# Attention in quarter tiles of the array, one bank for layer 1's first product, and a new order from re-priced rules

## The chip, the core and the metric

The kernel runs on one core of a Trainium2 chip. The metric is the device time of one execution in microseconds; of several executions the median counts.

## What is computed

Three stages follow each other. The first is a linear attention over B=4 sequences of S=768 tokens, H=8 heads of D=48 channels, with a decay per channel; its output, one row of 384 per token (3072 tokens), goes through two feed-forward layers with 2048 hidden units and different gates:

```python
state = np.zeros((B, H, D, D))
for t in range(S):
    cur = np.einsum('bhd,bhe->bhde', u[None] * kt, vt)
    y[:, :, t] = np.einsum('bhd,bhde->bhe', rt, state + cur)
    state = wt[:, :, :, None] * state + np.einsum('bhd,bhe->bhde', kt, vt)
...
h = x @ w_in;  g = np.maximum(h, 0.0) + alpha * np.minimum(h, 0.0);  x = g @ w_out
...
h = x @ w_in2; g = h * np.clip(h + 3.0, 0.0, 6.0) / 6.0;             out = g @ w_out2
```

All inputs are float32 except the weights, which arrive as float64 and are cut to float32 on the chip.

## The kernel before, in words

**The layers.** A *slot* is one block of 512 tokens (there are 6) with one of 16 blocks of 128 hidden units, so each layer has 96 slots. In a slot TensorE makes h (9 products `h<-xt,w` or `h<-x,w`: three blocks of 128 rows, each as three products of high and low parts, lines 765 to 767), ScalarE reads h into q, VectorE makes the gated value pg (line 808 in layer 1 from h and q, line 812 in layer 2), ScalarE rounds it to g's high part (line 818), VectorE or GpSimd makes the low part (line 821), and TensorE multiplies g with the second weight into three banks acc (9 products). The weights of a layer (16 x 2 pieces of 128x384) are loaded as float64 and taken apart by ScalarE (lines 95, 738) and by VectorE in two steps (wb, lines 98 and 103); the low part w (line 742) goes to VectorE or GpSimd. Layer 1's weights are made during its first block of tokens.

**The attention.** A *third* is 256 tokens of a sequence (there are 12; a sequence has three), a *unit* is a third of one pair of heads (48 units). Head 0 of a pair lies on partitions 0 to 47, head 1 on 64 to 111. For a unit SP loads k, r and w (`un`); VectorE scans w from the right to the products T (line 386), takes a floor of their first column (line 394) and its reciprocal (line 399) and scans to G (line 402); kr (line 423, VectorE or GpSimd) is k times T and r times G. A third also needs r*u*k summed over the channels (rk products, line 332, and the sums p, line 339). The unit's 256 tokens are two chunks of C=128. TensorE's work for a unit comes in two *visits* between the layers' products:

- the first visit makes the scores A (line 477, four 48x128x128 products, one for a chunk and head) and the transposes of k (line 484);
- then ScalarE copies the transposes (kT, line 509), makes four 128x128 diagonals X of p (line 458), and VectorE puts the scores of earlier tokens over X through a mask (line 499, line 494 for some early units);
- the second visit makes y from states and r (line 588, a block-diagonal 112x112 state for each chunk, which ScalarE fills with four 48x48 copies, line 538) and from X and v (lines 595 and 599), and then the products of kT and v for the next unit (lines 516 and 520); VectorE updates the running state Y (line 562).

y goes to the first layer's input xt as a high part (ScalarE, line 635) and a low part (VectorE, line 641).

**Banks.** PSUM has eight: three acc, two h, two for A (with kT's and the states' products behind the scores), one for y.

**The order.** Every step is declared to a planner (`class Plan`) with its engines and the cost on each, a due time in slots, the steps it waits for and the buffers it takes. The planner runs a list schedule on these costs: at each moment the engine that can begin first takes its ready step with the earliest due time. What comes out is the fixed order of each engine's queue. Costs have only this effect: the semaphores come from the dependencies. A step marked `pair=True` on VectorE takes turns with any step on GpSimd (`pair`, under LOCK). Units 0 to 7 (AHEAD) come before the first slot and borrow buffers of the layers; unit n is due U1 = 2 slots after unit n-1. Filler products on TensorE (`warm`) stand where it would idle before the first slot.

## Time and profile before

| what | us |
|---|---|
| median of 3 runs (944.52 to 947.65) | 946.64 |
| the profiled execution | 945.74 |
| its span, first to last instruction | 944.0 |
| TensorE busy | 920.3 |
| VectorE busy | 556.3 |
| ScalarE busy | 530.9 |
| GpSimd busy | 132.3 |

The profiled execution is one run with the hardware's instruction trace. Its span and its own time differ by what lies before the first and behind the last instruction. Busy time of an engine is the time in which it had an instruction; VectorE's instructions overlap their neighbours a little, so a step from start to start is shorter than a duration. TensorE's products overlap each other too: what one costs is the step to the next. A float32 product of the attention appears as two records, one of a layer as one.

### The profile page before, as it was taken

To read this page: it belongs to the slowest core of one execution; us is meant where nothing else is said; L and a number is where in the kernel's file an instruction comes from. 1 tells how busy PE (TensorE), PEld (TensorE's weight loads), DVE (VectorE), ACT (ScalarE), POOL (GpSimd) and SP (SyncE) were. 2 spreads that over 40 slices of the span, in tenths; PEclk is the share of its full clock that TensorE was granted. 3 is DMA by queue.
4 is the path that set the end of the run, shared out by engine and by line. 5 is a ranking of instruction groups with operands and counts; after the bars stand their busy time and mean duration, and the time that the engine had idled before them with its cause. 6 is when DMAs were issued, how large, how long until landed. Compare 5 with 4: busy or idle time off the path is not lost.

```text
span 944.0 us, 13745 instructions
## 1 busy us (share of the span) xinstructions
PE 920.3 (97%) x4914; PEld 743.2 (79%) x4914; DVE 556.3 (59%) x1087; ACT 530.9 (56%) x1266; POOL 132.3 (14%) x132
## 2 busy tenths in 40 slices
PE   7899989999999999999999999999999999999996
PEld 5677767878888788878888888888888888888885
DVE  8999997465655645564369886353353443443432
ACT  5998776565656655665378876363353453443331
POOL 4333234021121201100011130000000000000000
PEclk9999999999999999999999999999999999999998
DMA  8888214122312310110056530060140320500001
GB/s 250 256 268 283 81 52 145 55 79 70 107 64 57 109 55 31 58 64 7 9 186 197 175 111 1 1 200 1 54 147 1 123 79 1 172 30 1 34 1 38
DMA packets 36750, 86.20 MB, mean 91 GB/s; under 512 B 5056, under 2 KB 7488, under 8 KB 36672
## 3 DMA queue, kind: packets, MB, share of 16 engines
q1 hardware_dynamic: 36672, 85.22, 28.8%
q8 instruction: 41, 0.67, 0.3%
q14 instruction: 37, 0.30, 0.1%
HBM read 73.41 MB, written 9.44 MB: 88 GB/s over the span
## 4 chain that ended last, share of the span: by engine, by line
PE 82%; DVE 1%; DMA 0%; POOL 0%; issue 0%; POOLq 0%; DVEq 0%
PE acc L765 13%; PE acc L767 13%; PE acc L766 13%; PE h L765 12%; PE h L767 12%; PE h L766 12%; PE A L477 2%; PE y L595 1%; PE y L588 1%; PE A L484 1%; DMA rk<-in_tok 0%; PE y L599 0%; PE A L516 0%; POOL rk L332 0%; PE A L520 0%; DVE rk L332 0%
## 5 line engine op out<-in xcount | busy, mean ns | idle before, releaser
L765 PE MATMUL acc<-g,w 128*128 128x512 f32 x576 | 228.9, 397 | 0.0
L767 PE MATMUL acc<-g,w 128*128 128x512 f32 x576 | 224.6, 390 | 0.0
L766 PE MATMUL acc<-g,w 128*128 128x512 f32 x576 | 224.5, 390 | 0.0
L818 ACT ACTIVATE g<-pg 128x512 fp32r<-128x512 f32 x192 | 120.6, 628 | 137.7 <-PE acc L767 126.8
L821 DVE TENSOR_TENSOR g<-pg,g 128x512 fp32r<-128x512 f32 x176 | 121.7, 691 | 124.8 <-ACT g L818 124.7
L765 PEld LDWEIGHTS acc<-g,w 128*128 128x128 f32 x576 | 108.1, 188 | 23.4 <-issue 0.4
L767 PEld LDWEIGHTS acc<-g,w 128*128 128x128 f32 x576 | 108.1, 188 | 22.8
L766 PEld LDWEIGHTS acc<-g,w 128*128 128x128 f32 x576 | 108.2, 188 | 21.6 <-DVE g L821 0.3
L812 DVE SCALAR_TENSOR_TENSOR pg<-q,h 128x512 f32<-128x512 f32 x96 | 65.9, 686 | 98.6 <-ACT q L803 98.4
L808 DVE SCALAR_TENSOR_TENSOR pg<-h,q 128x512 f32<-128x512 f32 x96 | 66.1, 688 | 96.4 <-ACT q L801 96.3
L803 ACT ACTIVATE q<-h,three 128x512 f32<-128x512 f32 x96 | 65.8, 685 | 100.5 <-PE h L767 100.3
L765 PE MATMUL h<-xt,w 128*128 128x512 f32 x288 | 116.3, 404 | 1.2 <-ACT w L738 1.1
L767 PE MATMUL h<-xt,w 128*128 128x512 f32 x288 | 113.0, 392 | 0.9 <-POOL w L742 0.7
L766 PE MATMUL h<-xt,w 128*128 128x512 f32 x288 | 112.3, 390 | 0.0
L765 PE MATMUL h<-x,w 128*128 128x512 f32 x288 | 112.0, 389 | 0.0
L766 PE MATMUL h<-x,w 128*128 128x512 f32 x288 | 112.0, 389 | 0.0
L767 PE MATMUL h<-x,w 128*128 128x512 f32 x288 | 112.0, 389 | 0.0
L801 ACT ACTIVATE q<-h,nal 128x512 f32<-128x512 f32 x96 | 65.6, 684 | 73.6 <-PE h L767 71.7
L423 POOL TENSOR_TENSOR kr<-un,tg 112x512 f32<-112x512 f32 (+1 forms) x43 | 43.6, 1016 | 225.5 <-PE y L588 207.3
L765 PEld LDWEIGHTS h<-xt,w 128*128 128x128 f32 x288 | 54.9, 191 | 13.3 <-ACT w L738 2.2
L767 PEld LDWEIGHTS h<-xt,w 128*128 128x128 f32 x288 | 54.0, 188 | 14.1 <-DVE w L742 1.4
L766 PEld LDWEIGHTS h<-x,w 128*128 128x128 f32 x288 | 54.1, 188 | 11.3
(93 smaller groups left out, 1262.7 us busy)
## 6 DMA issues: line engine op xcount, KB each, us to landing
wraw<-in_w SPq DMA_DIRECT2D x64, 384.0 KB, 3.7
un<-in_unit SPq DMA_DIRECT2D x48, 337.3 KB, 3.2
raw<-in_w SPq DMA_DIRECT2D x32, 384.0 KB, 3.9
rk<-in_tok SPq DMA_DIRECT2D x24, 384.0 KB, 4.0
v<-in_vch SPq DMA_DIRECT2D x12, 384.0 KB, 3.1
x2d<-st SPq DMA_DIRECT2D x18, 256.0 KB, 2.1
x2r<-x2d SPq DMA_DIRECT2D x18, 256.0 KB, 4.6
out<-st SPq DMA_DIRECT2D x18, 256.0 KB, 3.5
```

What stands on the lines that cost most here:

```text
L423: eng[e].tensor_tensor(out=u["kr"][:, i].rearrange("p a (c s) -> p a c s", c=2), in0=u["in"][:, 0 : 2 * TH].rearrange("p (a c s) -> p a c ...
L477: nc.tensor.matmul(A[h][:, cs], kr[r0 : r0 + D, 0, cs], kr[r0 : r0 + D, 1, cs], start=True, stop=True,)
L484: nc.tensor.transpose(T[:, c, :], kr[:, 0, c * C : (c + 1) * C], ident[0:PR, 0:PR])
L765: nc.tensor.matmul(ps, whi, xhi, start=start, stop=False, skip_group_check=True)
L766: nc.tensor.matmul(ps, whi, xlo, start=False, stop=False, skip_group_check=True)
L767: nc.tensor.matmul(ps, wlo, xhi, start=False, stop=stop, skip_group_check=True)
L801: nc.scalar.activation(q, k["h"], AF.Relu, scale=nal[:, f : f + 1])
L803: nc.scalar.activation(q, k["h"], AF.Relu, bias=three)
L808: nc.vector.scalar_tensor_tensor(out=p, in0=k["h"], scalar=0.0, in1=k["q"], op0=ALU.max, op1=ALU.subtract)
L812: nc.vector.scalar_tensor_tensor(out=p, in0=k["q"], scalar=6.0, in1=k["h"], op0=ALU.min, op1=ALU.mult)
L818: nc.scalar.activation(k["g"][:, 0], k["p"], AF.Copy)
L821: eng[e].tensor_tensor(out=k["g"][:, 1], in0=k["p"], in1=k["g"][:, 0].bitcast(F32), op=ALU.subtract)
```

## The change

- **Chunks of 64.** A unit's two chunks j are each split into two sub-chunks p of Q=64 tokens. All products of the attention have at most 64 rows and 64 columns of weights, so that head h (rows) and sub-chunk p (output partitions) choose one of four quarters of the array. Scores within a sub-chunk are 64x64; what an earlier sub-chunk gives goes through states. A unit has 8 score products (N=64), 8 products with an identity in place of the transposes (N=48), 8 of keys and values (6 in the last third), 8 of values (N=64) and 8 of states (N=64; 6 in the first third).
- **States.** A half state U (line 621) and the full Y (line 639, one more VectorE instruction a chunk) are used directly as weights, 48x48 on the diagonal quarters; ScalarE scales one copy Z a chunk (line 600). The block-diagonal copies are gone.
- **X** is four diagonals of 64 columns, made by GpSimd in one instruction or by ScalarE in four; the triangle has 256 columns instead of 512.
- **Visits.** `visit` joins stages: from unit 17 on the states of unit n-1 and the scores of n are one visit, values and keys-values of n the other. A unit keeps its two banks (A, y or acc01) from scores to output.
- **Banks.** acc0 and acc1 become one tile of two banks, A and y have two each, h has one. From slot 80 on (FREE) h takes h, A and y in turn.
- **Layer 1's gate.** ScalarE copies h to q; VectorE makes pg = max(alpha*q, q) from q alone, so that h is read once. It is marked `pair`. A check that alpha is at most 1 is added at the end.
- **Scans.** The floor is gone; the first column is kept by a ScalarE copy. The early units' scans read their second input from a PSUM tile of zeros and ones (hz) and are not `pair`; the second scan is split in two there. kr and X have three buffers.
- **The planner.** Costs of most steps, a latency for each engine, a tail in which the next instruction may begin, and a queue for loads (ISSUE, FLIGHT, 1.26 a weight) are new numbers; LEAD makes units from 16 on due 7 slots ahead instead of 3.

```diff
-U0, U1, W0 = -3.9, 2.0, -0.82
+FREE = (NB - 1) * NF
+U0, U1, W0, LEAD = -3.9, 2.0, -0.82, 7.0
...
-    LATENCY = 0.08
-    SAME = {"PE": 0.0, "DVE": 0.1, "ACT": 0.15, "POOL": 0.1, "SP": 0.0}
+    TAIL = {"PE": 0.0, "DVE": 0.08, "ACT": 0.1, "POOL": 0.04, "SP": 0.0}
+    LATENCY = {"PE": 0.26, "DVE": 0.06, "ACT": 0.05, "POOL": 0.08, "SP": 0.0}
+    SAME = {"PE": 0.0, "DVE": 0.02, "ACT": 0.02, "POOL": 0.02, "SP": 0.0}
+    ISSUE, FLIGHT = 0.45, 1.6
...
-            free[e] = t + d
+            free[e] = t + d - self.TAIL[e]
...
-    ps_h = es.enter_context(tc.tile_pool(name="ps_h", bufs=2, space=PSUM))
+    ps_h = es.enter_context(tc.tile_pool(name="ps_h", bufs=1, space=PSUM))
...
+            if early:
+                starts = begin["t"][0:PR, 0 : 2 * C + 2]
+            else:
+                starts = restart.rearrange("p c s -> p (c s)")
             nc.vector.tensor_tensor_scan(
...
-                data1=restart.rearrange("p c s -> p (c s)")[:, ::-1], initial=0.0,
+                data1=starts[:, ::-1], initial=0.0,
...
-        def floor(e):
-            nc.vector.tensor_scalar(
-                fall[0:PR, n], u["T"][:, :, 0], 2.0**-60, None, op0=ALU.max
-            )
...
+        def scores():
+            pool = ps_acc if pair == "acc01" else ps_a
+            u["A"] = pool.tile([P, 2, TB], F32, tag=pair, name=f"A{n}")
+            ps = [u["A"][:, i] for i in range(2)]
+            u["ps"], kr = ps, u["kr"]
+            for w0, rhs in ((0, None), (C, ident2)):
+                for j in range(2):
+                    for p in range(2):
+                        for h in range(2):
+                            rows = slice(64 * h, 64 * h + D)
+                            cs = slice((2 * j + p) * Q, (2 * j + p + 1) * Q)
+                            r = kr[rows, 1, cs] if rhs is None else rhs[rows, 0:D]
+                            k0 = w0 + j * (Q if rhs is None else D)
+                            nc.tensor.matmul(
+                                ps[h][p * Q : (p + 1) * Q, k0 : k0 + r.shape[1]],
+                                kr[rows, 0, cs], r, start=True, stop=True,
+                            )
...
+        def states():
+            y = u["y"]
+            for j in range(2):
+                for h, p in ((0, 0), (1, 1), (0, 1), (1, 0)):
+                    if first and j == p == 0:
+                        continue
+                    rows = slice(64 * h, 64 * h + D)
+                    cs = slice((2 * j + p) * Q, (2 * j + p + 1) * Q)
+                    nc.tensor.matmul(
+                        y[rows, p, j * Q : (j + 1) * Q], u["S"][j, p]()[rows], u["kr"][rows, 1, cs],
+                        start=False, stop=True, skip_group_check=True,
+                    )
...
+        if n <= FUSE:
+            visit(d - 2, scores=n)
+        else:
+            visit(d - 2, states=n - 1, scores=n)
+        visit(d - 0.5, values=n, keysvalues=n)
+        if n < FUSE or n == NU - 1:
+            visit(d + 2, states=n)
...
-                nc.scalar.activation(q, k["h"], AF.Relu, scale=nal[:, f : f + 1])
+                nc.scalar.activation(q, k["h"], AF.Copy)
...
-                    out=p, in0=k["h"], scalar=0.0, in1=k["q"], op0=ALU.max, op1=ALU.subtract
+                    out=p, in0=k["q"], scalar=alp[:, f : f + 1], in1=k["q"],
+                    op0=ALU.mult, op1=ALU.max,
...
-        o_g = plan.op({"DVE": 0.62}, s + 0.8, gate, [o_q], new=[pb], use=[qb, hb])
+        o_g = plan.op(
+            {"DVE": 0.69}, s + 0.8, gate, [o_q], new=[pb], use=[qb] + ([hb] if m else []),
+            pair=(m == 0),
+        )
```

**TensorE's visits in layer 1.** Before, in the third block of tokens: the second visit of one unit with the keys-values of the next, and later a first visit (names: y, A the banks; kr, X, kT, sbd, v the operands; a number tells instances apart).

```order
L767 MATMUL h_2928<-xt_1846,w_5_0_1081 128x512
L588 MATMUL y_2941<-kr_2746,sbd_105 112x128
L595 MATMUL y_2941<-X_2751,v_2162 64x128
L599 MATMUL y_2941<-X_2751,v_2162 48x128
L516 MATMUL A_2886<-v_2551,kT_2910 64x48
L520 MATMUL A_2886<-v_2551,kT_2910 48x48
L765 MATMUL acc_2_0_2856<-g_2835,w_2_1_1054 128x512
...
L477 MATMUL A_2985<-kr_2960 128x128 x4
L484 MATMUL A_2985<-ident,kr_2960 128x112 x2
L765 MATMUL h_3001<-xt_1846,w_6_0_1178 128x512
```

Now, on the same engine, in the fourth block: values and keys-values of a unit behind one h, and behind the next h its states with the scores of the unit that follows.

```order
L840 MATMUL h_4991<-xt_3404,w_6_0_1511 128x512
L548 MATMUL A_4949<-X_4700,v_4026 64x64
L548 MATMUL A_4949<-X_4700,v_4026 48x64
...
L533 MATMUL A_4949<-v_4026,kT_4976 64x48
L533 MATMUL A_4949<-v_4026,kT_4976 48x48
...
L562 MATMUL A_4949<-kr_4885,U_0_5025 48x64 x2
L562 MATMUL A_4949<-kr_4885,Z_1_5049 48x64
...
L517 MATMUL A_5076<-kr_4983 64x64 x8
L517 MATMUL A_5076<-ident_91,kr_4983 64x48 x8
L838 MATMUL acc_3_4781<-g_4913,w_4_1_1515 128x512
```

The states moved from the second visit to the first, the keys-values stand with their own unit's values, and each product has become several of 64 columns or fewer.

**VectorE in the opening.** The first unit before, from its first scan (un the loaded unit, tg the scans, rk and p the sums over channels):

```order
L386 SCALAR_TENSOR_TENSOR tg_162<-un_142,restart 112x258
L394 TENSOR_SCALAR fall<-tg_162 112x2
L399 RECIPROCAL gfirst_109<-fall 112x2
L402 SCALAR_TENSOR_TENSOR tg_162<-un_142,gfirst_109 112x258
L332 TENSOR_TENSOR rk_147<-rk_147 128x384
L423 TENSOR_TENSOR kr_167<-un_142,tg_162 112x256
```

and now:

```order
L402 SCALAR_TENSOR_TENSOR tg_161<-un_137,hz 112x258
L412 RECIPROCAL tg_161<-tg_161 112x2
L423 SCALAR_TENSOR_TENSOR tg_161<-un_137,tg_161,hz 112x127 x2
L457 TENSOR_TENSOR kr_169<-un_137,tg_161 112x256
L344 TENSOR_TENSOR rk_139<-rk_139,u_sb 128x384
```

The floor is out, hz in PSUM has taken the place of restart and gfirst, and the second scan is two.

**VectorE in layer 1's first block of tokens.** Before, around the 11th and 12th gate (wb the steps of a weight, w its low part):

```order
L103 SCALAR_TENSOR_TENSOR wb_11_1_1605<-wraw_11_1_1227,wb_11_1_1605 128x384
L808 SCALAR_TENSOR_TENSOR pg_1626<-h_1534,q_1565 128x512
L394 TENSOR_SCALAR fall<-tg_112 112x2
L808 SCALAR_TENSOR_TENSOR pg_1638<-h_1607,q_1630 128x512
L399 RECIPROCAL gfirst_110<-fall 112x2
L742 TENSOR_TENSOR w_11_1_1635<-wb_11_1_1605,w_11_1_1635 128x384
L821 TENSOR_TENSOR g_1643<-pg_1626,g_1643 128x512
```

and now, around the same weight:

```order
L105 SCALAR_TENSOR_TENSOR wb_11_1_2121<-wraw_11_1_1688,wb_11_1_2121 128x384
L457 TENSOR_TENSOR kr_2144<-un_1810,tg_108 112x512
L414 RECIPROCAL gfirst_105<-tg_107 112x2
L678 TENSOR_TENSOR x_3_2134<-A_1953,x_3_2134 112x256
L886 SCALAR_TENSOR_TENSOR pg_2179<-q_1943,alp 128x512
L430 SCALAR_TENSOR_TENSOR tg_107<-un_1949,gfirst_105 112x258
L568 COPY_PREDICATED X_1867<-mask_92,A_2161 128x256
L815 TENSOR_TENSOR w_11_1_2146<-wb_11_1_2121,w_11_1_2146 128x384
```

The gates read q and alpha instead of h and q, and a unit's scan, kr and triangle have come among them. Between the first and the 17th gate VectorE has 104 instructions of two SBUF inputs before (27 and 28 steps and 20 low parts of weights, 15 scans, 8 low parts of g and 6 kr) and 125 now (52 steps and 20 low parts of weights, 16 scans, 12 low parts of g, 8 kr, one rk product and 16 gates). GpSimd has 26 there now: 8 low parts of weights, 10 rk products, 4 low parts of g, 3 diagonals and one kr.

## Rows read from the trace of the kernel before

**Rows 1.** The page, part 1: busy time, share of the span and count of instructions of each engine.

```profile
PE 920.3 (97%) x4914; PEld 743.2 (79%) x4914; DVE 556.3 (59%) x1087; ACT 530.9 (56%) x1266; POOL 132.3 (14%) x132
```

**Rows 2.** The table of stretches. Columns: stretch in us from the span's start, its length, busy time and (count) of TensorE's matmuls (PE), its weight loads (PEld), VectorE (DVE), ScalarE (ACT) and GpSimd (POOL), granted TensorE clock, mean busy share of the DMA engines, GB/s. The first is from layer 1's first gate to its 17th, the second lies in the middle of layer 1.

```profile
58.00:143.00 85.00, 80.17 (x468) 60.27 (x468) 80.86 (x168) 68.15 (x176) 25.20 (x22) 1.00 0.53 167
...
200.00:300.00 100.00, 100.00 (x610) 80.21 (x609) 58.02 (x123) 58.95 (x159) 17.41 (x16) 1.00 0.23 73
```

**Rows 3.** The instructions of VectorE in order of time: start, duration in us, engine, line, operation, output<-input, shapes. The first gate of layer 1 and the 17th (in brackets the idle time ahead of it and what ended that).

```profile
57.99 0.67 DVE L808 SCALAR_TENSOR_TENSOR pg<-h,q 128x512 f32<-128x512 f32 x1
...
142.84 0.69 DVE L808 SCALAR_TENSOR_TENSOR pg<-h,q 128x512 f32<-128x512 f32 x1 [0.99 <-ACT q L801]
```

**Rows 4.** The same view of GpSimd and of VectorE between 55 and 57 us: a kr on the one, the low part of a weight on the other.

```profile
55.12 1.27 POOL L423 TENSOR_TENSOR kr<-un,tg 112x512 f32<-112x512 f32 x1 [1.29 <-issue]
...
55.35 1.45 DVE L742 TENSOR_TENSOR w<-wb,w 128x384 fp32r<-128x384 f32 x1
```

**Rows 5.** The same view of VectorE from 59 to 62 us, where GpSimd has no instruction. Nothing stands idle between them, so that the step from start to start is the time that one takes the engine.

```profile
59.05 0.54 DVE L98 SCALAR_TENSOR_TENSOR wb<-wraw,wa 128x384 int32<-128x384 int32 x1
59.52 0.68 DVE L386 TENSOR_TENSOR_SCAN tg<-un,restart 112x258 f32<-112x258 f32 x1
60.12 0.53 DVE L103 SCALAR_TENSOR_TENSOR wb<-wraw,wb 128x384 int32<-128x384 int32 x1
...
61.04 0.68 DVE L821 TENSOR_TENSOR g<-pg,g 128x512 fp32r<-128x512 f32 x1
61.64 0.54 DVE L742 TENSOR_TENSOR w<-wb,w 128x384 fp32r<-128x384 f32 x1
```

**Rows 6.** The groups of VectorE's instructions by line and shape, from 58 to 143 us. Columns: line, engine, operation, output<-input, output<-input shapes, count | busy us, mean ns of one | idle us before them and what ended it.

```profile
L98 DVE SCALAR_TENSOR_TENSOR wb<-wraw,wa 128x384 int32<-128x384 int32 x27 | 16.7, 644 | 1.9 <-issue 1.9
...
L103 DVE SCALAR_TENSOR_TENSOR wb<-wraw,wb 128x384 int32<-128x384 int32 x28 | 15.3, 574 | 0.0
...
L808 DVE SCALAR_TENSOR_TENSOR pg<-h,q 128x512 f32<-128x512 f32 x17 | 11.6, 681 | 1.0 <-ACT q L801 1.0
...
L742 DVE TENSOR_TENSOR w<-wb,w 128x384 fp32r<-128x384 f32 x20 | 11.3, 587 | 0.0
...
L386 DVE TENSOR_TENSOR_SCAN tg<-un,restart 112x258 f32<-112x258 f32 x8 | 6.5, 806 | 0.0
...
L821 DVE TENSOR_TENSOR g<-pg,g 128x512 fp32r<-128x512 f32 x8 | 5.4, 677 | 0.0
...
L423 DVE TENSOR_TENSOR kr<-un,tg 112x512 f32<-112x512 f32 x6 | 5.1, 848 | 0.0
...
L402 DVE TENSOR_TENSOR_SCAN tg<-un,gfirst 112x258 f32<-112x258 f32 x7 | 4.7, 675 | 0.0
```

**Rows 7.** TensorE's matmuls in order of time, layer 1: the first visit of a unit (L477 scores, L484 transposes, left out of these rows) between matmuls of the layers. L765 to L767 are the three products of a layer's step.

```profile
201.28 0.39 PE L766 MATMUL acc<-g,w 128*128 128x512 f32 x1
201.51 0.39 PE L767 MATMUL acc<-g,w 128*128 128x512 f32 x1
...
201.82 0.71 PE L477 MATMUL A<-kr 48*128 48x128 f32 x8
...
202.65 0.47 PE L765 MATMUL h<-xt,w 128*128 128x512 f32 x1
...
202.97 0.39 PE L766 MATMUL h<-xt,w 128*128 128x512 f32 x1
```

**Rows 8.** The same view, 7 us later: a second visit (L588 states; L595 and L599 values, the two column halves; L516 and L520 keys-values, 64 and 48 columns), between matmuls of the layers.

```profile
208.67 0.39 PE L767 MATMUL h<-xt,w 128*128 128x512 f32 x1
208.90 0.60 PE L588 MATMUL y<-kr,sbd 112*112 112x128 f32 x4
...
209.43 0.31 PE L595 MATMUL y<-X,v 128*48 128x128 f32 x1
209.44 0.31 PE L599 MATMUL y<-X,v 128*48 128x128 f32 x1
...
209.91 0.21 PE L516 MATMUL A<-v,kT 128*64 128x48 f32 x1
209.91 0.21 PE L520 MATMUL A<-v,kT 128*48 128x48 f32 x1
...
210.04 0.21 PE L520 MATMUL A<-v,kT 128*48 128x48 f32 x1
...
210.06 0.22 PE L516 MATMUL A<-v,kT 128*64 128x48 f32 x1
210.22 0.50 PE L765 MATMUL acc<-g,w 128*128 128x512 f32 x1
...
210.56 0.39 PE L766 MATMUL acc<-g,w 128*128 128x512 f32 x1
```

**Rows 9.** The same view at 55 us: a visit of keys-values alone (L520's rows left out).

```profile
55.17 0.39 PE L767 MATMUL h<-xt,w 128*128 128x512 f32 x1
...
55.49 0.26 PE L516 MATMUL A<-v,kT 128*64 128x48 f32 x1
...
55.74 0.50 PE L765 MATMUL h<-xt,w 128*128 128x512 f32 x1
...
56.08 0.39 PE L766 MATMUL h<-xt,w 128*128 128x512 f32 x1
```

**Rows 10.** The page, part 5: ScalarE's first read of layer 1's h (columns as in rows 6).

```profile
L801 ACT ACTIVATE q<-h,nal 128x512 f32<-128x512 f32 x96 | 65.6, 684 | 73.6 <-PE h L767 71.7
```

458 lines of the change are left out of this document (247 added, 211 removed).

## The prediction

> **What bounds the kernel now.** I read the busy line of the page first, then the table of stretches, then the order of the instructions, then single visits of TensorE to the attention. TensorE is busy for 920.3 of 944.0 us [rows 1]. The table separates two regimes. From 200 to 300 us TensorE is busy for all of 100.00 us and VectorE for 58.02: there the time is TensorE's alone, and it stays so to the end. From 58 to 143 us three things are full at once: TensorE 80.17 of 85, VectorE 80.86, and GpSimd has 25.20 us in 22 instructions [rows 2]. This is the first token block of layer 1, from its first gate (the VectorE instruction that makes pg) at 57.99 to its 17th at 142.84, 84.85 us [rows 3]; VectorE prepares that layer's 32 weights in it beside the attention.
>
> VectorE and GpSimd get in each other's way there: the weight's low part on VectorE, started behind a GpSimd kr at 55.12, took 1.45 us [rows 4], where one of its length takes 0.47 from start to start when GpSimd is still [rows 5]. The gate (h in PSUM, q in SBUF) averages 681 ns over the block [rows 6], about its length undisturbed; the scan averages 806 [rows 6] against 0.68 undisturbed [rows 5]. So VectorE instructions with two SBUF inputs and GpSimd's take turns, and those with one input in PSUM do not. I call this turn-taking the port.
>
> **Part 1, the opening (before the first gate).** By the order, the 16 scans of the eight early units now take their second input from a tile of zeros in PSUM, and the 12 floor instructions are gone: 28 instructions leave the port. What each waits is the scan's 806 less 0.68 us, 0.13; 28 x 0.13 = 3.6. New VectorE work (state sums Y, split scans) and a halved triangle about cancel. Bounds: 0 (GpSimd does more in the opening, 29 reading instructions instead of 20, and may hold others) and twice the gain, -7. I take **-4**, the row's own value rounded.
>
> **Part 2, the first block (first to 17th gate).** Port time before, counts and lines from [rows 6], lengths from [rows 5]: 55 weight steps and 20 low parts at 0.47 = 35.3; 15 scans at 0.60 = 9.0; 8 low parts of g at 0.60 = 4.8; 6 kr of the same size 3.6; sum 52.7. With GpSimd's 25.2 it is 77.9 of 84.85. After, counts from the order between the same gates: 52 + 20 weight steps 33.8; 16 scans 9.6; 12 low parts of g 7.2; 8 kr 4.8; one rk 0.5; and the 16 gates, which now read q twice from SBUF and so join the port, 9.6: sum 65.5. GpSimd does 26, of which three are the new diagonals of 256 elements; 23 at its mean 1.15 (25.20 / 22) and three at half of it give 28. Together 93.5. TensorE needs about 84 in this block either way (16 slots of 18 matmuls at 0.23, 66, and some 18 for the visits, at the prices of part 3), so the port becomes the limit. If it is filled without a gap the block takes 93.5, **+8.7**. The lower end is 0: a gate that reads one tile twice is shown by no row, and off the port it leaves 83.9, TensorE's time. The upper end is the fill of before, 77.9 / 84.85 = 92%: 101.8, +17. I take the middle value because in the block of before TensorE shared the limit, and here it does not.
>
> **Part 3, TensorE's visits from the 17th slot on.** A visit is what stands between two matmuls of the layers; these start 0.23 apart. First visit before (scores, two transposes): 201.51 to the second matmul behind it, 202.97, is 1.46; two regular steps are 0.46; cost 1.00 [rows 7]. Second visit (states, values, and the keys-values of the next unit): 208.67 to 210.56 less 0.46 is 1.43 [rows 8]. Where a unit has one transpose, two keys-values products or one state product less, I take off 0.1, 0.11 and 0.21 from the same rows' paces. From the order 17 first visits at 1.00, 12 at 0.9, and 10, 12 and 8 second ones at 1.43, 1.31 and 1.22, one last at 1.22: 68.9 us.
>
> A visit of keys-values alone (four records, two at once) cost 56.08 - 55.17 - 0.46 = 0.45 [rows 9]; its two steps of 0.055, the pace below, off it leave **0.34** to get in and out. In [rows 8] two column halves of the array run side by side (209.43 and 209.44), and the half with 64 columns starts a record each 0.05 (209.91 to 210.06 in three steps) while the one with 48 needs 0.13 for three: each tile goes at its own pace. I price the new quarter tiles by the slower, 0.055 a record of 64 columns. A new first visit has 32 records of scores and transposes on four tiles (8 each, 0.44) and 16 of states on two (0.44; the first third of a batch 12, 0.33): 1.22 or 1.11. A new second visit has 16 of values and 16 of keys-values on four: 0.44, with the 0.34 it is 0.78. The order has 21 at 1.22, 8 at 1.11, 29 at 0.78, one at 0.78: 57.9. **-11.0.** Bounds come with the rivals.
>
> **What I cost at nothing.** One bank for h: the next first product must wait for ScalarE's q, 684 ns [rows 10]; from slot 7 to 79 the order has over 2.0 us of other TensorE work between two first products, and later slots have three banks. If ScalarE ran late by 1 us in ten of the 80 slots it would cost 10. Layer 2 and the end keep their instructions. ScalarE loses work (four diagonals, four block copies a unit) but does not set the end. Loads have the same bytes; units are due four slots sooner, and their loads and rk products move ahead with them on SP's and GpSimd's queues (the products are in part 2's counts; the DMA share of 0.53 in the first block [rows 2] leaves room for the loads).
>
> **Sum.** -4 + 8.7 - 11.0 = -6.3. The profiled execution took 945.74, its span 944.0 and 1.74 around it: 939.4. It lies 0.9 under the median of the runs, 946.64, which with the same difference gives **940.3, rounded 940**.
>
> **Rivals.**
>
> *A, slower: the quarter tiles don't pay.* The new visits from slot 16 on hold 2304 records against 59 x 0.34 = 20.1 us of entry. They equal the 68.9 of before at (68.9 - 20.1) / 2304 = 21 ns a record, and with parts 1 and 2 the change breaks even at 19; my sum has 16. The densest stretch of [rows 8] has eight records from 209.91 to 210.06, 21 ns. If records can't be fed faster, visits cost +0.8 and the time is 952; if only two tiles run at a time, 0.055 / 2 = 27.5 ns, +14.6 and 966. Against it: neighbours in different tiles start 10 ns apart, and the two halves hold different paces, which a common feed would not allow. No row shows four tiles.
> The Trainium skill, "TensorE: Matmul & The Clock Gate", section "Back-to-back issue gap", gives products of up to 64 columns an issue floor of about 25 ns each; by that the visits are an estimated 77.7 us and the time 960. The 10 ns between neighbours in [rows 8] speak against it across tiles, the 21 ns of the run of eight nearly for it.
>
> *B, no gain: the port.* With the fill of before the first block takes 101.8: -4 + 17 - 11 = +2, 948.6.
>
> *C, more gain: the first block isn't stretched* (the gate stays off the port): -4 + 0 - 11 = -15, 931.6; and if scores start on tiles that the states leave free, up to 0.22 for each of 29 visits, another 6: 925.
>
> **How the numbers follow.** The forecast has 0.50, its own range 930 to 947; A 0.16 (952 to 966), B 0.12 (945 to 952), C 0.22 (918 to 932). The range 922 to 955 leaves out about 0.10 of A and 0.05 of C. A measurement tells 0.3%, 2.8 us, from no change. Below 943.8: 0.43 of the forecast and C, 0.65. Within: 0.07 of each of the forecast and B, 0.14. Above 949.5: A and the rest of B, 0.21.
>
> **What would show it.** In the changed profile, visits from 200 us on of 1.2 and 0.8 us, with four records starting within some 0.03 us (A: visits of 1.5 and 1.1 or more); the first gate at about 54; the 17th 93 us behind it (B: over 100; C: about 85), with gates far over 681 ns where GpSimd runs; VectorE full and TensorE below its 80 of 85 between them; no waits of first products for q. Wrong altogether would be a TensorE that is no longer full between 200 and 450 us: then a chain across engines, which I cost at nothing, sets the pace.

## The result

The changed kernel takes 957.46 us (median of 4 executions, 955.50 to 965.45); the kernel before took 947.14 beside it. The ratio is 1.0130, 95% interval 1.0098 to 1.0161. The forecast was 940, with a range that ended at 955. The profiled execution of the changed kernel took 958.08, its span is 956.2, against 944.0 before: +12.2 where the sum said -6.3. Split at gates of both traces (a gate is the VectorE instruction that makes pg):

| stretch | before, us | forecast | measured |
|---|---|---|---|
| start to layer 1's first gate | 57.99 | -4 | +2.7 |
| first to 17th gate | 84.85 | +8.7 | +12.7 |
| 17th gate to layer 2's 17th | 462.31 | -11.0 | -9.7 |
| layer 2's 17th gate to its 77th | 244.80 | 0 | 0.0 |
| its 77th to its 96th, the last | 77.88 | 0 | +6.1 |
| last gate to the end | 16.13 | 0 | +0.5 |

So TensorE's gain came nearly as priced, and three places took it back and more: the opening, the first block, and a place near the end of which the forecast said nothing.

### The profile page after: what moved, and what is told of

The parts are those of the page before. It is cut to its first block, busy times and chain, and to the rows that moved or that the text cites. A ratio compares the mean times of both kernels' runs of the same rounds, so it can differ in the third digit from the quotient of the medians.

```text
span 956.2 us, 18506 instructions
## 1 busy us (share of the span) xinstructions
PE 917.9 (96%) x7341; PEld 738.4 (77%) x7341; DVE 582.2 (61%) x1160; ACT 478.7 (50%) x1200; POOL 128.1 (13%) x120
## 4 chain that ended last, share of the span: by engine, by line
PE 83%; DVE 6%; DMA 4%; issue 3%; ACT 2%; POOL 1%; SPq 1%; DVEq 0%; ACTq 0%; POOLq 0%
PE acc L838 13%; PE h L838 13%; PE acc L839 13%; PE h L839 13%; PE h L840 13%; PE acc L840 13%; DMA un<-in_unit 4%; PE A L517 2%; PE A L562 1%; PE A L548 1%; SPq L690 1%; DVE pg L886 1%; PE A L533 1%; DVE tg L402 1%; DVE wb L105 1%
## 5 line engine op out<-in xcount | busy, mean ns | idle before, releaser
L900 DVE TENSOR_TENSOR g<-pg,g 128x512 fp32r<-128x512 f32 x177 | 124.2, 701 | 126.1 <-ACT g L897 125.8
L838 PE MATMUL h<-xt,w 128*128 128x512 f32 x288 | 117.6, 408 | 10.3 <-ACT q L879 10.1
L839 PE MATMUL h<-xt,w 128*128 128x512 f32 x288 | 114.3, 397 | 0.0
L840 PE MATMUL h<-xt,w 128*128 128x512 f32 x288 | 114.1, 396 | 0.0
L886 DVE SCALAR_TENSOR_TENSOR pg<-q,alp 128x512 f32<-128x512 f32 x96 | 75.7, 789 | 37.6 <-ACT q L879 37.1
L879 ACT ACTIVATE q<-h 128x512 f32<-128x512 f32 x96 | 56.9, 592 | 78.6 <-PE h L840 78.5
L838 PEld LDWEIGHTS h<-xt,w 128*128 128x128 f32 x288 | 55.1, 191 | 24.3 <-ACT q L879 12.2
L838 PEld LDWEIGHTS h<-x,w 128*128 128x128 f32 x288 | 54.5, 189 | 13.6 <-DVE pg L891 2.0
L840 PEld LDWEIGHTS h<-xt,w 128*128 128x128 f32 x288 | 55.1, 191 | 12.2
L839 PEld LDWEIGHTS h<-xt,w 128*128 128x128 f32 x288 | 55.2, 192 | 10.7
```

What stands on the lines that cost most here:

```text
L838: nc.tensor.matmul(ps, whi, xhi, start=start, stop=False, skip_group_check=True)
L839: nc.tensor.matmul(ps, whi, xlo, start=False, stop=False, skip_group_check=True)
L840: nc.tensor.matmul(ps, wlo, xhi, start=False, stop=stop, skip_group_check=True)
L879: nc.scalar.activation(q, k["h"], AF.Copy)
L886: nc.vector.scalar_tensor_tensor(out=p, in0=k["q"], scalar=alp[:, f : f + 1], in1=k["q"], op0=ALU.mult, op1=ALU.max,)
L900: eng[e].tensor_tensor(out=k["g"][:, 1], in0=k["p"], in1=k["g"][:, 0].bitcast(F32), op=ALU.subtract)
```

## The profile after

Its first line, answering [rows 1]: TensorE is busy for 2.4 us less in a span 12.2 us longer, VectorE for 25.9 us more.

```profile
PE 917.9 (96%) x7341; PEld 738.4 (77%) x7341; DVE 582.2 (61%) x1160; ACT 478.7 (50%) x1200; POOL 128.1 (13%) x120
```

The two gates that answer [rows 3], in VectorE's instructions in order of time, and the two stretches of [rows 2] (columns as there):

```profile
60.68 0.72 DVE L886 SCALAR_TENSOR_TENSOR pg<-q,alp 128x512 f32<-128x512 f32 x1
...
158.22 0.72 DVE L886 SCALAR_TENSOR_TENSOR pg<-q,alp 128x512 f32<-128x512 f32 x1
```

```profile
60.68:158.22 97.54, 82.67 (x861) 62.35 (x862) 92.52 (x188) 63.72 (x175) 31.05 (x23) 0.93 0.47 151
200.00:300.00 100.00, 99.44 (x1082) 78.58 (x1081) 66.85 (x141) 49.86 (x152) 16.21 (x12) 1.00 0.25 78
```

In the first block VectorE has an instruction for 92.52 of 97.54 us, as before for 80.71 of 84.85. TensorE is no longer near full there (82.67 of 97.54), and its granted clock is 0.93 where it was 1.00. From 200 us on TensorE is full again. The groups of VectorE in that block answer [rows 6]:

```profile
L886 DVE SCALAR_TENSOR_TENSOR pg<-q,alp 128x512 f32<-128x512 f32 x17 | 13.8, 810 | 0.0
L815 DVE TENSOR_TENSOR w<-wb,w 128x384 fp32r<-128x384 f32 x20 | 13.4, 683 | 0.9 <-ACT w L811 0.9
L402 DVE TENSOR_TENSOR_SCAN tg<-un,restart 112x258 f32<-112x258 f32 x9 | 10.2, 1132 | 0.0
...
L568 DVE COPY_PREDICATED X<-mask,A 128x256 f32<-128x256 uint8 x8 | 3.5, 436 | 1.7 <-ACT kT L576 1.7
L621 DVE SCALAR_TENSOR_TENSOR U<-Y,tg,A 112x48 f32<-112x48 f32 x12 | 3.0, 261 | 0.9 <-PE A L533 0.7
L639 DVE TENSOR_TENSOR Y<-U,A 112x48 f32<-112x48 f32 x15 | 2.9, 197 | 0.3
```

The scan's mean rose from 806 to 1132 ns: more of the scans wait for GpSimd (four take 1.49 or 1.50 us, before one did). The gate's mean rose from 681 to 810, but few gates wait. Their line (duration in ns, shortest, median and longest):

```profile
L886 DVE SCALAR_TENSOR_TENSOR pg<-q,alp x17: 718/742/1503, 60.7 to 158.2; 128x512 f32<-128x512 f32 x17
```

Only three of the 17 are over 0.75 us (0.87, 1.09 and 1.50), 1.3 us in all over 0.74; the others are a little longer than before because of their own length, 0.74 for 0.68. New are the many short sums U and Y, and small waits for ScalarE's kT and TensorE's products.

TensorE's visits answer [rows 7, 8]. In order of time, the first visit of a unit after a sequence's first third (L562 states, L517 scores and copies of k), and a second visit 4 us later:

```profile
232.54 0.39 PE L840 MATMUL acc<-g,w 128*128 128x512 f32 x1
232.86 0.36 PE L562 MATMUL A<-kr,U 48*48 48x64 f32 x5
...
233.23 0.40 PE L517 MATMUL A<-kr 48*64 48x64 f32 x14
233.41 0.44 PE L517 MATMUL A<-ident,kr 48*64 48x48 f32 x16
233.78 0.50 PE L838 MATMUL acc<-g,w 128*128 128x512 f32 x1
234.12 0.39 PE L839 MATMUL acc<-g,w 128*128 128x512 f32 x1
...
236.41 0.39 PE L840 MATMUL h<-xt,w 128*128 128x512 f32 x1
236.73 0.46 PE L548 MATMUL A<-X,v 64*64 64x64 f32 x16
237.00 0.41 PE L533 MATMUL A<-v,kT 64*48 64x48 f32 x16
237.34 0.50 PE L838 MATMUL acc<-g,w 128*128 128x512 f32 x1
237.67 0.39 PE L839 MATMUL acc<-g,w 128*128 128x512 f32 x1
```

By the forecast's own measure they cost 234.12 - 232.54 - 0.46 = 1.12 (forecast 1.11) and 237.67 - 236.41 - 0.46 = 0.80 (0.78). Of the 21 full first visits behind the 17th gate the shortest and the median are 1.23 (1.22). Rival A, that quarter tiles don't pay, is out. From the first of the second visit's 32 records to the next product of a layer it is 0.61 us, 19 ns a record with the pipeline's filling. The Trainium skill's floor of about 25 ns ("TensorE: Matmul & The Clock Gate", section "Back-to-back issue gap") does not hold here, across four tiles.

Near the end, TensorE between two blocks of tokens of layer 2 (order of time; in brackets the idle time and what ended it):

```profile
878.86 0.39 PE L840 MATMUL acc<-g,w 128*128 128x512 f32 x1
881.83 0.19 PE L1015 MATMUL cnt<-ones,chk_s 128*1 128x1 f32 x2 [2.58 <-DVE chk_s L1009]
882.26 0.80 PE L838 MATMUL h<-x,w 128*128 128x512 f32 x1 [0.24 <-DVE flag L1018]
882.85 0.63 PE L839 MATMUL h<-x,w 128*128 128x512 f32 x1
...
885.54 0.40 PE L840 MATMUL h<-x,w 128*128 128x512 f32 x1
887.50 0.50 PE L838 MATMUL h<-x,w 128*128 128x512 f32 x1 [1.56 <-DVE pg L891]
```

The next block's first h waits for the count of the check (cnt), which has its bank y, the count for VectorE's reductions, and these for the drain of the block before (VectorE drains from 878.61 and reduces from 880.41 to 881.77); then products start 0.43 apart instead of 0.23 (granted clock from 882.3 to 884.9 us: 0.50), and the pipeline from h to gate has to fill again.

## The experiments

Gates are read from one profiled execution each; the time is a median. How far such a reading can be trusted: `end` has the changed kernel's order up to 837 us, and its 17th gate came 2.4 us sooner, layer 2's 17th 1.1 us later; `a_ybuf` has it up to 125 us, and its first gate came 1.7 us later. The ratio is to the kernel before, run beside it.

| run | time, us | ratio, 95% interval | first gate | 17th | layer 2's 17th |
|---|---|---|---|---|---|
| before | 946 to 947 | 1 | 57.99 | 142.84 | 605.15 |
| the change | 957.46 | 1.0098 to 1.0161 | 60.68 | 158.22 | 610.79 |
| end | 953.40 | 1.0058 to 1.0113 | 59.08 | 155.80 | 611.93 |
| lead3 | 955.47 | 1.0054 to 1.0108 | 61.29 | 154.02 | 607.38 |
| e_lead3 | 945.79 | 0.9967 to 1.0006 | 60.96 | 153.61 | 606.77 |
| e_lead1 | 940.85 | 0.9914 to 0.9954 | 62.93 | 144.18 | 601.55 |
| b_lead7 | 954.31 | 1.0061 to 1.0107 | 58.48 | 151.59 | 612.19 |
| b_gate | 955.56 | 1.0069 to 1.0111 | 58.45 | 149.86 | 615.26 |
| b_bank | 955.19 | 1.0059 to 1.0144 | 57.23 | 147.34 | 613.55 |
| a_nopair | 960.76 | 1.0131 to 1.0200 | 53.58 | 155.81 | 612.06 |
| a_gate | 957.53 | 1.0068 to 1.0140 | 54.45 | 155.81 | 609.35 |
| e_lead3_h | 944.58 | 0.9963 to 0.9993 | 59.97 | 152.63 | 603.77 |
| e_lead3_hn | 946.28 | 0.9989 to 1.0026 | 53.33 | 151.21 | 602.55 |
| e_lead1_h | 944.39 | 0.9964 to 0.9989 | 58.52 | 148.97 | 600.31 |
| a_scan | 965.00 | 1.0156 to 1.0238 | 67.30 | 162.68 | 615.34 |
| a_ybuf | 960.66 | 1.0100 to 1.0169 | 62.42 | 159.74 | 615.75 |
| a_plan | 967.16 | 1.0193 to 1.0242 | 59.72 | 173.12 | 618.59 |
| b_plan7 | 966.05 | 1.0177 to 1.0223 | 64.41 | 156.34 | 628.76 |
| e_lead3_plan | 956.04 | 1.0057 to 1.0116 | 64.10 | 167.89 | 618.56 |

### The check at the end

```diff
+        if j == NB - 2:
+            seen = list(plan.ops)
         for f in range(NF):
             add_slot(1, j, f)
+            if j == NB - 1 and f == 3:
+                add_check(NB * NF + (NB - 1) * NF + 4)
...
-        o = plan.op({"DVE": 0.7}, due, ok, list(plan.ops))
+        o = plan.op({"DVE": 0.7}, due, ok, list(seen))
```

> The changed kernel; only the check at the end is declared later (inside the last block of tokens) and depends on the steps known before the block ahead of it. Up to 860 us every engine keeps its order. Theory 1, the check's bank: the first products h of the last block had to wait for the count in bank y, the count for VectorE's reductions, and these for the drains of the block before; from the last product ahead of it to the first regular h behind it this cost 6.1 us (stall, a half clock for some products, the pipeline's refill). Without it the time falls by 5.5 to 6.5 us, to about 951.4, and the 81st gate of layer 2 stands about 6 us behind that of the kernel before, not 20. Rival: the stall comes from the drains and the change of x there, whatever the check does; then the time falls by less than 1 us.

Layer 2's 77th to last gate takes 77.88 us again (84.03 in the change), and TensorE is busy for all of 870 to 890 us (15.62 of 20 in the change). The span of the profiled execution fell by 5.1 us (a wait of TensorE at 257 us, 0.56 in the change, was 2.46 here), the median by 4.1, short of the 5.5 expected. Theory 1 holds, the rival is out.

### The lead

`lead3` is the change and `e_lead3` is `end` with the first edit, `e_lead1` is `end` with 1.0 in its place, and `b_lead7` is the kernel before with the second.

```diff
-U0, U1, W0, LEAD = -3.9, 2.0, -0.82, 7.0
+U0, U1, W0, LEAD = -3.9, 2.0, -0.82, 3.0
...
-        return (U0 + U1 * (n - AHEAD)) if n < 2 * AHEAD else 2.0 * (n - AHEAD) - 3.0
+        return (U0 + U1 * (n - AHEAD)) if n < 2 * AHEAD else 2.0 * (n - AHEAD) - 7.0
```

> The changed kernel with LEAD back at 3 instead of 7. Theory 2, too much work moved ahead: loads of units stand on SP's queue among the weights' (one took 11.3 us from 53.5 us) and VectorE gets their scans inside the first block; without the lead the 17th gate of layer 1, at 158.2 in the changed kernel, comes 4 us sooner or more and the time falls to about 953. Rival (the gates set the pace of the first block, not the units): VectorE has only 2 us less work between the first and the 17th gate, the 17th gate moves by 2 us or less, and the time stays within 2 us of 957.5.

> The changed kernel with the check declared later (as in the run end) and LEAD at 3. If what the two runs showed adds up (6 us at the end; 4.2 us at the 17th gate, 2 to 3.4 of them kept to layer 2), the time is between 948 and 950. If LEAD's gain was a matter of the one execution that was profiled, 953.

> As e_lead3 (945.8; 17th gate at 153.6), with LEAD at 1. Theory 2, work moved ahead: two slots less lead take another 2 us or more off the first block, 17th gate at 151 or before, and the time falls to 943 or less. Rival: with LEAD at 3 the units are no longer ahead of need; at 1 their scores come late, TensorE waits ahead of them behind the 17th gate, and the time is 945 or more.

> The kernel before with units from 16 on due 7 slots ahead instead of 3, nothing else. Theory 2, work moved ahead into a block in which VectorE is full: the 17th gate comes 3 us or more later than 142.8, and the time is 949 or more. Rival: the lead hurts only with the new visits, whose keys-values and states hang on one another; 17th gate within 1.5 us of 142.8, time within 2 of 946.

With 3 the 17th gate came 4.2 us sooner, on the theory's side of the line, but the time fell by 2.0 us only, to 955.47 and not the 953 expected. Layer 2's 17th gate came 3.4 us sooner, and the check then cost more: 86.28 us from layer 2's 77th to its last gate, 8.4 over the kernel before, where the change has 6.1. The sum of both edits, 945.79, is better than foreseen, 7.6 us under `end`. With 1 the kernel takes 940.85 and beats the kernel before by 0.46 to 0.86%. From `end` to `e_lead1`, by LEAD alone, the time fell by 12.5 us. And the lead alone, in the kernel before, costs 8 us: 954.31 against 946.54. The table of stretches, from the first to the 17th gate, for the kernel before, `b_lead7` and `e_lead1`:

```profile
57.99:142.84 84.85, 80.02 (x467) 60.13 (x467) 80.71 (x167) 68.00 (x176) 25.04 (x22) 1.00 0.53 167
```

```profile
58.48:151.59 93.11, 84.46 (x487) 63.34 (x486) 88.14 (x177) 71.12 (x184) 34.67 (x26) 0.96 0.48 155
```

```profile
62.93:144.18 81.25, 72.75 (x699) 55.15 (x700) 79.48 (x165) 58.23 (x157) 21.16 (x14) 1.00 0.53 165
```

Only a constant differs between `b_lead7` and the kernel before: VectorE is busy for 88.14 us instead of 80.71 and GpSimd for 34.67 instead of 25.04, and the block is 8.26 us longer. In `e_lead1` VectorE is busy for 79.48 (the change: 92.52) and GpSimd for 21.16 (31.05). In all four VectorE is busy for about 95% of the block or more: the block lasts as long as what the order puts on VectorE and GpSimd in it.

What fell from `end` to `e_lead1` is mostly scans (16 to 11, 14.2 to 8.7 us) and low parts of weights (20 to 19, 14.5 to 10.4 us, so mostly their waits for GpSimd); sums, kr, p and triangles fell by 5.2 us together. VectorE's busy time holds its waits for GpSimd, so these rows do not part a limit by all of VectorE's instructions from one by the turns alone.

What is not done there costs VectorE nothing behind it, where it is busy for 58 to 67 us in 100. TensorE's visits of the units that moved behind the 17th gate come on top there: against the change 9.2 of the 14.0 us at that gate are left at layer 2's 17th, against `end` 10.4 of 11.6.

A rival fell with this: that late loads hold VectorE in the block. A unit's load at 53.47 did take 11.31 us among the weights' (in the chain of waits of the change), but in that block VectorE idles ahead of its scans for 0.0 us (L402 above).

### The gate's turns and the one bank, each alone in the kernel before

```diff
-                nc.scalar.activation(q, k["h"], AF.Relu, scale=nal[:, f : f + 1])
+                nc.scalar.activation(q, k["h"], AF.Copy)
...
-                    out=p, in0=k["h"], scalar=0.0, in1=k["q"], op0=ALU.max, op1=ALU.subtract
+                    out=p, in0=k["q"], scalar=alp[:, f : f + 1], in1=k["q"],
+                    op0=ALU.mult, op1=ALU.max,
```

> The kernel before with one part of the change alone: ScalarE copies h to q and layer 1's gate is max(alpha*q, q) from q, so that it reads SBUF twice; the order of every engine stays as it was. Theory 3, the port: the 16 gates of the first block join the turn-taking, 52.7 + 9.6 + 25.2 = 87.5 us of turns; the stretch from the first to the 17th gate grows from 84.85 to between 87.5 (no gap) and 95 (the fill of before, 92%), the time by 3 to 10 us. Rival (such a gate takes no part in the turns, or VectorE's own time decides): the stretch stays within 1 us of 84.85 and the time within 2 us of 946.6.

The order is the same, and the block grew from 84.85 to 91.41. VectorE's gate and GpSimd's kr in it (groups as in [rows 6], 681 and 1263 ns before):

```profile
L808 DVE SCALAR_TENSOR_TENSOR pg<-q,alp 128x512 f32<-128x512 f32 x17 | 17.9, 1051 | 0.0
```

```profile
L423 POOL TENSOR_TENSOR kr<-un,tg 112x512 f32<-112x512 f32 x1 | 4.2, 4218 | 4.3 <-PE acc L767 4.3
```

The gates' 17.9 us are 6.3 more than before, the block's 6.6 us nearly by themselves. That a gate which reads one tile twice takes part in the turns was shown by no row before; here it is: seven of the 17 take 1.00 to 2.53 us, the others 0.73 to 0.75. The Trainium skill ("GPSIMD Engine Reference", section "1. Specifications") says that GpSimd contends with VectorE instructions of two SBUF inputs; the run agrees. Not foreseen: 3.1 us more were lost behind the 17th gate, where TensorE waited ahead of scores seven times, 2.9 us in all.

`b_bank` adds one bank for h up to slot 79, freed by q, and two by two tags behind it:

```diff
-        hb, qb, pb, gb = plan.buf("h", 2), plan.buf("q", 2), plan.buf("pg", 2), plan.buf("g", 3)
+        where = "h" if s < (NB - 1) * NF else ("h", "h2")[s % 2]
+        hb, qb, pb, gb = plan.buf(where, 1), plan.buf("q", 2), plan.buf("pg", 2), plan.buf("g", 3)
...
-        o_g = plan.op({"DVE": 0.62}, s + 0.8, gate, [o_q], new=[pb], use=[qb, hb])
+        o_g = plan.op({"DVE": 0.62}, s + 0.8, gate, [o_q], new=[pb], use=[qb] + ([hb] if m else []))
```

> The kernel before with the new gate of layer 1 (from q alone, as in b_gate) and one bank for h up to slot 79, freed when ScalarE has copied h to q; two banks later. It is compared with b_gate (955.6, 91.4 us from the first to the 17th gate). Theory 5, the bank: in the changed kernel layer 1's first products waited 10.1 us for ScalarE's q, all of it time lost; then this kernel loses 5 us or more against b_gate in the first block (97 us or more) and takes 960 or more. Rival: these waits of TensorE lie beside VectorE's work, which sets that block's length; the stretch stays within 2 us of 91.4 and the time within 2.5 of 955.6.

90.11 us and 955.19: in the kernel before one bank costs nothing measurable. But TensorE waited for q there for 3.3 us only. That its 10 us of such waits in the change lie beside VectorE's work fits VectorE's 92.52 of 97.54 us; no run gave the changed kernel a second bank in that block.

### The gate in the changed kernel

`a_gate` and `e_lead3_hn` have the whole edit, `a_nopair` its last line alone, `e_lead3_h` and `e_lead1_h` all but that line.

```diff
-                    out=p, in0=k["q"], scalar=alp[:, f : f + 1], in1=k["q"],
+                    out=p, in0=k["h"], scalar=alp[:, f : f + 1], in1=k["q"],
...
-            {"DVE": 0.69}, s + 0.8, gate, [o_q], new=[pb], use=[qb] + ([hb] if m else []),
+            {"DVE": 0.69}, s + 0.8, gate, [o_q], new=[pb], use=[qb, hb],
-            pair=(m == 0),
+            pair=False,
```

> The changed kernel with pair=False on layer 1's gate: the same instructions, but the planner no longer makes the gate take turns with GpSimd's steps, so the order is another. Theory 4, the planner's rule puts the gates late: in the changed kernel q of the first slot was ready at 54.25 us and its gate began at 60.68, behind GpSimd's four rk products; by the order 3.9 us of VectorE's work now stand behind the first gate that stood ahead of it. Then the first gate comes at 57 or sooner, the 17th 4 us sooner than 158.2 or more, and the time falls to about 953. Rival, the port itself: the gates wait for GpSimd in the hardware whatever the order; the first gate may come sooner, but the 17th stays within 2 us of 158.2.

> The changed kernel with layer 1's gate as max(alpha*h, q), h from PSUM, not marked pair: its order is that of a_nopair but for a few steps, the gate reads SBUF once, and h's one bank is held until the gate has run. Compared with a_nopair (960.8; 102.2 us from the first to the 17th gate). Theory 3, the port: 16 x 0.6 us leave the turns; the stretch falls by 6 to 10 us, to 92 to 96, and the time to about 952. Rival, the bank: the next first product waits for the gate as well, and what the port gives the bank takes back: stretch 100 or more, time 958 or more, and TensorE with new gaps ahead of h behind 160 us.

> As e_lead3 (945.8; first to 17th gate 92.65 us), with layer 1's gate as max(alpha*h, q), h from PSUM; the planner's pair mark stays. Theory 3, the port: the gates leave the turns, VectorE and GpSimd are busy for 5 us less in the first block, and the 17th gate comes at 149 or before; time 942 or less. Rival, the bank: h is held until the gate has run, TensorE waits instead; 17th gate at 152 or later, time 945 or more.

> As e_lead3_h, without the pair mark, so that the planner does not make the gate take turns with GpSimd either. Theory 4 (the mark puts gates late): first gate 6 us sooner than in e_lead3_h, and the 17th sooner by 3 us or more. Rival: the first gate comes sooner and VectorE's other work follows it; the 17th gate within 2 us of that of e_lead3_h.

> As e_lead1 (940.85; 17th gate at 144.2), with layer 1's gate from h in PSUM and q, the pair mark kept. Theory 3, the port: VectorE is still busy for 79.6 of the block's 81.3 us, so taking the gates out of the turns brings 2 us or more; 938.9 or less. Rival, the bank or nothing to gain: 940 or more.

The mark does put the first gate late: without it it comes at 53.3 to 54.5, 6.6 to 7.1 us sooner. But the 17th gate moves by 1.4 to 2.4 us only and the time does not fall (960.76, 946.28): theory 4 is right on the gate and wrong on the time. What VectorE has not done before the first gate it does behind it.

Taking the gate out of the turns brought 3.2 us (`a_gate` against `a_nopair`) and 1.2 (`e_lead3_h` against `e_lead3`), with intervals that overlap, and with LEAD at 1 it cost 3.5, with intervals that do not. So the 9 us that the gate's turns cost the kernel before are not there to be had back in the changed kernel. The traces say why. What gates of the first block took over 0.74 us comes to 5.3 us in `b_gate` (seven gates), but to 2.7 in `a_nopair` (five), 2.5 in `e_lead3` (five) and 1.2 in `e_lead1` (two). What costs the 3.5 stays open: in these three h's bank is held until the gate has run, and the order differs too, with 178 VectorE instructions in `e_lead1_h`'s block instead of 164; the two profiled executions, 942.55 and 942.91, don't show it.

### The opening

VectorE's share in it, from the table of stretches up to the first gate, before and then in the change:

```profile
0.00:57.99 57.99, 48.33 (x441) 35.57 (x441) 53.98 (x139) 45.02 (x152) 24.59 (x37) 0.97 0.79 241
```

```profile
0.00:60.68 60.68, 52.25 (x1050) 40.44 (x1050) 50.83 (x147) 35.10 (x131) 34.60 (x50) 0.92 0.78 243
```

It is busy for 3.2 us less and idle for 5.8 more. 3.3 us of the idle time, none before, are waits of the sums Y that a product of the states (L562) ended, and 3.0, 1.4 before, are waits for loads of units. `a_scan` has the first two edits (the order stays as in the change), `a_ybuf` the last:

```diff
-                starts = begin["t"][0:PR, 0 : 2 * C + 2]
+                starts = restart.rearrange("p c s -> p (c s)")
...
-                        data1=begin["t"][0:PR, 0 : C - 1], initial=u["tg"][:, 1, i0 : i0 + 1],
+                        data1=restart[:, 0, 0 : C - 1], initial=u["tg"][:, 1, i0 : i0 + 1],
...
-                yb = plan.buf(f"Y{pr}", 2)
+                yb = plan.buf(f"Y{pr}", 4)
```

> The changed kernel in its own order; only the scans of the eight early units read their second input from SBUF (restart) again, not from PSUM, so that 24 VectorE instructions return to the turn-taking. Theory of the forecast's part 1: each then waits 0.13 us or more for GpSimd, the first gate comes 3 to 4 us later than at 60.7, at 64, and the time grows by the same. Rival: the opening is set by loads and by the chain from engine to engine, VectorE has 9.8 us of idle time in it, and the scans' waits lie there; the first gate moves by less than 1.5 us and the time by less than 2.

> The changed kernel with four buffers instead of two for the states Y of each pair. Theory 6: TensorE now reads U and Y as weights, so that Y's buffer is not free until the states' products have run; VectorE waited 0.96 + 2.03 + 0.29 us for that in the first 25 us, in its own queue, with scans behind it. With four buffers the first gate comes 2 to 3 us sooner than 60.7 and the 17th sooner than 158.2 by as much, the time falls to about 955. Rival: the opening's end hangs on loads and on the order; the first gate stays within 1 us of 60.7.

The scans' groups from 0 to 60 us, in the change and then in `a_scan`:

```profile
L423 DVE TENSOR_TENSOR_SCAN tg<-un,tg,hz 112x127 f32<-112x127 f32 x16 | 6.7, 461 | 0.1
L402 DVE TENSOR_TENSOR_SCAN tg<-un,hz 112x258 f32<-112x258 f32 x8 | 5.3, 677 | 1.6 <-DMA un<-in_unit 1.6
```

```profile
L423 DVE TENSOR_TENSOR_SCAN tg<-un,tg,restart 112x127 f32<-112x127 f32 x16 | 13.4, 876 | 0.1
L402 DVE TENSOR_TENSOR_SCAN tg<-un,restart 112x258 f32<-112x258 f32 x12 | 12.8, 1076 | 2.1 <-DMA un<-in_unit 2.1
```

Back in the turns the scans take 1.6 to 1.9 times as long (four of the twelve in the last row are those of later units, on `restart` in both), the first gate comes 6.6 us later and the time is 7.5 us longer, more than the 3 to 4 expected. This is not what the change gained over the kernel before. `a_scan` keeps an order that was made without turns for these scans. The order before was made with them, and its scans ahead of the first gate (up to 57.9 us) waited little:

```profile
L386 DVE TENSOR_TENSOR_SCAN tg<-un,restart 112x258 f32<-112x258 f32 x12 | 9.0, 754 | 1.4 <-DMA un<-in_unit 1.4
L402 DVE TENSOR_TENSOR_SCAN tg<-un,gfirst 112x258 f32<-112x258 f32 x12 | 8.2, 690 | 0.1
```

Theory 6 falls, but otherwise than by its rival. VectorE's waits for Y up to 60.6 us, in the change and in `a_ybuf` (total us, times, longest):

```profile
DVE Y L639 <- PE A L562: 3.3, 3, 2.0
DVE Y L639 <- PE A L562: 3.0, 3, 2.2
```

Four buffers did not take the wait away, so it is not for the buffer (first gate +1.7, time +3.2). Whether the time hangs on it, no run tested.

### The planner's rules

`a_plan` (from the change) and `e_lead3_plan` carry the planner class of the kernel before, `b_plan7` is the kernel before with the new class and LEAD 7. The edit is the whole class; its core, for the first two:

```diff
-    TAIL = {"PE": 0.0, "DVE": 0.08, "ACT": 0.1, "POOL": 0.04, "SP": 0.0}
-    LATENCY = {"PE": 0.26, "DVE": 0.06, "ACT": 0.05, "POOL": 0.08, "SP": 0.0}
-    SAME = {"PE": 0.0, "DVE": 0.02, "ACT": 0.02, "POOL": 0.02, "SP": 0.0}
-    ISSUE, FLIGHT = 0.45, 1.6
+    LATENCY = 0.08
+    SAME = {"PE": 0.0, "DVE": 0.1, "ACT": 0.15, "POOL": 0.1, "SP": 0.0}
```

> The changed kernel's instructions, ordered by the rules of the planner before (one latency of 0.08, no tails, no load queue, half speed of TensorE up to 9.5 us); costs of the steps, due times and LEAD as in the change. Theory 7, the new rules: the order that they give puts the gates and loads of the first block badly; under the old ones the first gate comes before 57 and the 17th 5 us sooner than 158.2 or more, and the time is 952 or less. Rival: the instructions set the length, in any order; the 17th gate stays within 2 us of 158.2 and the time between 954 and 961.

> The kernel before, its instructions as they were, ordered by the changed kernel's rules and with LEAD at 7 (costs of the steps as before). Theory 7, the new rules: the 17th gate comes at 148 or later instead of 142.8 and the time is 950 or more. Rival: an order of these rules does no harm to other instructions; 17th gate within 2 us of 142.8, time within 2.5 of 946.3.

> As e_lead3, ordered by the planner's rules before. Theory 7: another 4 us or more off e_lead3, so 945 or less, which is under the kernel before. Rival: the time of e_lead3 within 2 us.

Theory 7 falls. The old rules make the changed kernel 10 us slower, and the new ones the old kernel 20 (8 of them by the lead, from `b_lead7`). Each set of rules does better with the instructions that it came with. In `a_plan` the difference arises in the first block (113.4 us). In `b_plan7`, against `b_lead7`, it does not: that block is 1.2 us shorter, the opening 5.9 longer and the stretch from the 17th gate to layer 2's 17th 11.8 longer.

## Why the prediction was wrong

By medians the miss is 17.2 us (957.46 for 940.3). Two things that the forecast costed at nothing make 11.7 of it, each undone by an edit of its own: the check at the end, 4.1 (`end`), and the four slots of lead, 7.6 (`e_lead3` against `end`). The other 5.5 are left in `e_lead3`, which has the lead of the kernel before: in its profiled execution the first gate comes 3.0 us later (forecast -4), its first block is 7.8 longer (+8.7), the stretch behind it 9.2 shorter (-11.0). What is off there is the opening above all.

**Part 3, the visits: right.** 1.23, 1.12 and 0.80 us for forecasts of 1.22, 1.11 and 0.78; -9.7 for -11.0 in the stretch. The difference is about what TensorE waited for triangles (X) of units at three places, 1.4 us.

**Part 2, the first block, with the lead costed at nothing: a step that failed.** It took VectorE's turns with GpSimd as the limit, put the growth down to the 16 gates, and let the four slots of lead pass with the counts of two-input steps and the words on loads and rk products. +12.7 came for +8.7, inside the bounds of 0 and 17, but from other steps, so that the size came near partly by chance. Between the gates VectorE is busy for 11.8 us more. By sums of durations the sums U and Y gave +3.8, low parts of g +3.6, scans +3.0, the gates +2.2, low parts of weights +1.9 and p +1.6; weight steps, floors and triangles gave -5.5. Much of it is the lead: from LEAD 7 to 1 the block fell by 15.5 us (`end` to `e_lead1`), from 7 to 3 by 4.1 (`end` to `e_lead3`), and the lead alone gave the kernel before +8.3. That the gate joins the turns was right (`b_gate`), but its 9.6 us were 6.6 in the one kernel where it could be isolated, and in the change the gates' time grew by 2.2 only. VectorE as a whole was full before, too. Whether all its instructions or the turns alone are the limit stays open: the forecast's own sum, with what GpSimd was busy, is 52.7 + 25.0 = 77.7 of 84.85 us before and 65.5 + 31.1 = 96.6 of 97.54 in the change, the waits of GpSimd counted in.

**Part 1, the opening: a step that failed, the sign of the term.** The first gate came 2.7 us later, not 4 sooner. The waits that the term counted were there to be saved: ahead of the first gate of the kernel before, 24 scans took about 1.0 us over 0.69 each and 12 floors 2.4 over 0.16, together near the 3.6 of the sum. VectorE's busy time up to the first gate did fall, from 54.0 to 50.8 us, in part because other work now stands behind that gate. But its idle time, which the term left out, rose from 4.0 to 9.9, for Y and for loads above all (what the time loses by each, the runs did not settle). And the planner's pair mark on the gate put it behind other steps: q was ready at 54.25, sooner than the 56.66 of before, and the gate began at 60.68. The forecast took the first gate for the end of the opening; it is only a place in VectorE's queue (53.6 without the mark, at a later total).

**The end: a step that failed, costed at nothing: 6.1 us.** "Layer 2 and the end keep their instructions" was true but for a check of alpha; the bank of one of them was shared with h from then on, and a wait came of it. The order shows it: the count stands ahead of the block's first h, and before it stood between an h and the products of another slot.

**One bank for h: at nothing, which is right in the kernel before** (`b_bank`) and not tested in the changed one. The sign given for it, no waits of first products for q, did not come: there were 10 us of such waits.

**The rivals.** A is out by the visits. B named the place, but by the port's fill and to 948.6. C did not happen. The sign for "wrong altogether", TensorE not full between 200 and 450 us, did not come either: the loss lay before 160 us and behind 878. Undoing the check and the added lead gives 945.79, no clear gain over the kernel before. 940.85 needs a lead of 1, two slots under the kernel before. That this is the forecast's time is chance: its opening is 4.9 us longer than before, its first block 3.6 shorter and the stretch behind it 4.9 shorter, where -4, +8.7 and -11.0 were forecast.

## What to carry to other kernels

Where an engine beside the bottleneck is full in one stage and half idle in the next, work moved ahead into the full stage is lost time however early it makes its results: price every instruction that a due time moves, on the engine that is full there, not only those of the kind under study. A first event of a stage is no measure of the stage before it; compare the time by which the same work is done. When a buffer gets a second user, look who else has it, as far as the last lines of the program.

## What the hardware showed that I had not expected

- A GpSimd product among VectorE's two-input steps can take several times its length: kr 4.22 us in `b_gate` (1.26 before), and in the change a low part of a weight 2.63 (1.01 else) and one of g 3.03 (1.30 before).
- A VectorE step with one small SBUF input waits for GpSimd, too: ahead of the first gate of the kernel before five of the 12 floors (112x2) took 0.53 to 0.96 us, each beside a GpSimd instruction, the others 0.14 to 0.17.
- A gap of TensorE of 4.2 us at 108 us in the change costs it twice: behind it the granted clock is at the lower level, 1.2 GHz. The table of stretches:

```profile
108.00:112.00 4.00, 0.36 (x12) 0.21 (x8) 4.00 (x9) 2.22 (x7) 1.04 (x1) 0.79 0.31 94
112.00:116.00 4.00, 3.44 (x8) 2.77 (x9) 4.00 (x8) 2.19 (x5) 0.64 (x1) 0.50 0.00 0
```

From 112 to 116 us TensorE is busy at a granted clock of 0.50 and gets 8 products done, where 4 us hold 17 at full clock.
